# An earlier and thinner token list between attention and a mixture of experts

## The chip, the cores and the metric

The program runs on one core of a Trainium2 chip, in one launch. A core has five engines that run their own queues in order: TensorE (PE in the profile; its weight loads are PEld), VectorE (DVE), ScalarE (ACT), GpSimd (POOL) and SyncE (SP, which here only issues DMAs and reads a few registers). The metric is the device time in microseconds (us), the median of several runs.

## The reference

```python
def _attn_ref(q, k, v):                      # q, k, v: 8 x 8 x 1152 x 64
    q_pool = q.reshape(B, H, S // 2, 2, D).mean(axis=3)
    scores = np.matmul(q_pool, k.transpose(0, 1, 3, 2)) / np.sqrt(D)
    attn = np.exp(scores - scores.max(-1)); attn /= attn.sum(-1) + 1e-09
    return np.matmul(attn, v)
def _moe_ref(x, modality_id, w_gate, modality_bias, w1, w2):   # x: 4608 x 512, 8 experts of 1024
    logits = x @ w_gate + modality_bias[modality_id]
    e_idx = np.argmax(logits, axis=1)        # one expert for each token
    gate_w = softmax(logits)[tokens, e_idx]
    for e in range(E):
        mask = e_idx == e
        out[mask] = gate_w[mask, None] * (np.maximum(x[mask] @ w1[e], 0.0) @ w2[e])
```

Attention runs for 64 heads with pooled queries; its 4608 output rows are the tokens, and each goes through the one expert that its gate picks.

## The kernel before

**Attention.** The 64 heads are worked as 32 pairs (two heads side by side on the 128 partitions). The loop in `attention` has 18 steps a pair. Each step issues scores, the low halves of the exponentials, value products of earlier scores, and the maxima of the pair to come. For the reader of the trace: `L903`/`L904` are the score products, `L905` the exponentials on ScalarE (24 a pair), `L886`/`L888` the low halves `Pl` on ScalarE and VectorE, `L962` to `L964` the value products, `L836`/`L837` the maxima of the next pair (product, then VectorE reduction), `L803` the row of maxima, `L807` its transpose on TensorE and `L817` the DMA that puts the row in place.

What a later pair needs is prepared a pair or two ahead: GpSimd adds the query halves (`L655`), casts them (`L664`), takes the differences `lo` (`L692`, three a pair) and scales the values to `VH` (`L783`, two a pair: half 1 at step 3, half 0 at step 4). VectorE makes `VS` (`L795`, step 6) and `vl` (`L779`) from `VH`. Four of these GpSimd instructions are held: `hold` makes them wait for a certain VectorE instruction, so that they don't run beside it.

**Order.** The engines PE, ACT, DVE and POOL run in the order in which the code issues, step by step; SP's DMAs are ordered by a scheduler, unless `issue_after` puts one behind another. The list `side` holds generators (`route`, `first_list`, `other_list`); each is taken up after the one before it has ended, one `yield` at a time, at the end of a step. The number yielded is the count of steps to the next piece.

**Routing and lists.** Tokens come in four groups of eight pairs each. When a group is complete, `route(g)` picks each token's expert (one hot in `oh`), its gate (`gt`, stored to DRAM) and its place among its expert's tokens (`pos`). After the third group's routing `first_list` runs: the first `NA` = 6 blocks of 256 tokens are given to experts (`first_blocks`, `ownA`: the owner of each block), `place` works out each token's row in its block, and `listing` turns the rows into a list of token numbers by products of one-hot matrices (`ol`: which lane, `r`: which column). It works over 3 x 9 columns of 128 tokens. What is left of it when the last pair begins is drained in `gather_first`, just ahead of the first gather.

**Experts.** A block gathers its tokens from DRAM (`gather_x`, two indirect DMAs on GpSimd), multiplies by the first weights (`gemm1`) and the second (`gemm2`), and scatters. The first block's tokens and its four first weight quarters are fetched during attention's last pairs, into buffers of attention (`raw...`): `gather_first` and `load_first`, at the steps `T_G0` and `T_W0` counted from the start of pair 31. Their split into halves runs at the steps `T_W1` = (6, 4, 10, 11) of pair 31. The owner of a block is read by SP from `ownA` (`value_load`).

Of the kernel before, what the change touches and what calls it, by code (L numbers as in the profile page):

```python
# [42 lines left out]
BANK = W3 // 4  # L43
T_LIST = -127
PL = 2
RS = (4, 4, 2, 2)
SLOW_P = 1
# [41 lines left out]
JOBS = (8,)  # L89
T_G0 = -1  # L90
T_X0 = 7
# [27 lines left out]
NF = 4  # L119
T_W0 = (1, 3, 2, 3)  # L120
W1D = 0
# [42 lines left out]
class Router:  # L164
# [11 lines left out]
    def setup(self, ids, w_gate, bias):  # L176
# [40 lines left out]
        nc.sync.dma_start(out=self.xs[T - NT * P:T, DM:XW].rearrange("(t p) d -> p t d", p=P), in_=z)  # L217
        self.pos = con.tile([P, NTT], F32, name="pos")
        self.exp = con.tile([P, NTT], F32, name="exp")

# [56 lines left out]
    def route(self, g, eng):  # L277
# [45 lines left out]
        nc.vector.tensor_scalar(gt[:, :, 0], gt[:, :, 0], ts2[:, 0:1], 1.0 / WSC ** 2, op0=ALU.mult, op1=ALU.mult)  # L323
        nc.gpsimd.tensor_copy(gt[:, :, 1], ts2[:, 1:2].broadcast_to([P, NT]))
        eng.dma_start(out=self.xs[g * NT * P:(g + 1) * NT * P, DM:XW].rearrange("(t p) d -> p t d", p=P), in_=gt)
        yield rs
# [126 lines left out]

    def place(self, nt, late):

        nc, sm = self.nc, self.sm
        be = lambda a: a.unsqueeze(1).broadcast_to([P, nt, E])
        yield
        wide = lambda i: sm.tile([P, nt, E], F32, name=f"ohp{nt}_{i}") if late else sm.tile([P, 3, NT, E], F32, name=f"wide{i}").rearrange("p q t e -> p (q t) e")
        oh = wide(0)  # L460
# [13 lines left out]
        yield from pick(lim, self.na)  # L474
        yield from pick(row, self.full if late else self.cumA[:, 0:E])
        nc.vector.tensor_tensor(row, row, self.pos[:, 0:nt], op=ALU.add)
        if late:
            yield from pick(ok, self.done)
            nc.vector.tensor_tensor(ok, self.pos[:, 0:nt], ok, op=ALU.is_ge)
            more = new("more")  # L480
            yield from pick(more, self.half)
            nc.vector.tensor_tensor(more, more, ok, op=ALU.mult)
            nc.vector.tensor_tensor(row, row, more, op=ALU.add)
        nc.vector.tensor_tensor(ok, self.pos[:, 0:nt], lim, op=ALU.is_ge if late else ALU.is_lt)
        yield
# [13 lines left out]
        yield  # L499
        nc.vector.tensor_single_scalar(self.hi, self.hi, -float(2 * T // P), op=ALU.add)  # L500

    def operands(self, g, n, out):
# [63 lines left out]
    def first_list(self):  # L566

        for _ in self.first_blocks():
            yield 1
        for _ in self.place(3 * NT, False):  # L570
            yield PL
        yield T_LIST
        acc = self.con.tile([P, 2, 2 * NA], F32, name="accA")
        yield from self.listing(3, 2 * NA, acc)
        self.idxA = self.indices(2 * NA, acc, "A")

    def other_list(self):
        yield from self.other_blocks()
        yield from self.place(4 * NT, True)
        acc = self.con.tile([P, 2, 2 * (NBF - NA) + E], F32, name="accB")  # L580
        yield from self.listing(4, 2 * (NBF - NA) + E, acc)
        self.idxB = self.indices(2 * (NBF - NA) + E, acc, "B")


def attention(tc, ctx, att, ident, npairs, xpool, on_two, on_split, on_scale, jobs, side, set_pm, started, ahead, hip):
# [213 lines left out]
    def row(p, mp, u0, u1):  # L799

        n = u1 - u0
        m9 = sm.tile([P, 9], F32, name="m9")
        nc.vector.tensor_reduce(m9[:, 0:n], mp[:, u0:u1], op=ALU.max, axis=AX.X, negate=True)  # L803

        def finish():
            pt = some(0) if p else small()
            nc.tensor.transpose(pt[0:n, 0:P], m9[:, 0:n], ident)  # L807
            if now[0] > NSTEP:
                later_end(FD, lambda: put(pt))
            else:  # L810
                put(pt)

        def put(pt):
            mr = sm.tile([9, P], F16, name="mr", bufs=1)
            made.add((p, f"row{u1}"))
            nc.vector.tensor_scalar(mr[0:n], pt[0:n, 0:P], 1.0 / ROW, 16.0 * math.log(PSC) / ROW, op0=ALU.mult, op1=ALU.add)
            done = (nc.sync if p or u0 else nc.scalar).dma_start(out=B2[p % 2][D:D + 1, 2 * S + u0 * P:2 * S + u1 * P], in_=mr[0:n])  # L817
            if turns:
                with tc.issue_after(done.ins):
                    while turns:  # L820
                        turns.pop(0)()
        return finish
# [172 lines left out]

    turns = []
    now, flushed = [0], [-1]
# [133 lines left out]
    if ahead:  # L1131
        last = (npairs - 1) * NSTEP
        room = []

        def early():
# [37 lines left out]
    for t in range(NSTEP * npairs, NSTEP * npairs + 40):  # L1173
# [4 lines left out]
        ends(t)  # L1178
    assert not any(todo.values()) and not any(at_end.values())


# [10 lines left out]
def gather_x(nc, rt, j, tile_):  # L1192

    x = []
    for h in parts(j):
        x.append(tile_(h))
        nc.gpsimd.indirect_dma_start(out=x[h][:, :], out_offset=None, in_=rt.xs[0:3 * NT * P if j < NA else T, :],
                                     in_offset=bass.IndirectOffsetOnAxis(ap=index(rt, j, h)[0], axis=0))
    return x
# [22 lines left out]

def experts(tc, ctx, rt, ident, pre, w1, w2, out, side, first):

# [43 lines left out]
    def load_w(j, q):  # L1268
# [3 lines left out]
        if e is None:  # L1272
            own, k = (rt.ownA, j) if j < NA else (rt.ownB, j - NA) if j < NBF else (rt.ownH, j - NBF)
            e = b["e"] = nc.sync.value_load(own[0:1, k:k + 1], min_val=0, max_val=E - 1)
        if q < 4:
# [249 lines left out]
def attention_moe(tc, att, ids, w_gate, bias, w1, w2, out):  # L1525
    nc = tc.nc
    with ExitStack() as ctx:
# [9 lines left out]
        def on_two(n, x2):  # L1537
# [29 lines left out]
        def load_first(q, tile_):  # L1567
            if not q:
                first["e"] = nc.sync.value_load(rt.ownA[0:1, 0:1], min_val=0, max_val=E - 1)
# [10 lines left out]
        with ExitStack() as c2:  # L1580
            c2.enter_context(tc.manual_schedule(engines=MANUAL))
            attention(tc, c2, att, ident, NPAIR, xpool, on_two, on_split, rt.token_scale, jobs, side, set_pm, lambda: rt.setup(ids, w_gate, bias), ahead, hip)
# [6 lines left out]
        experts(tc, ctx, rt, ident, pre, w1, w2, out, rest(), first)  # L1589

# [43 lines left out]
```

## Time and profile before

| what | us |
|---|---|
| median of 3 runs | 1129.57 |
| runs, lowest and highest | 1128.46, 1130.51 |
| the profiled execution | 1128.8 |
| its span, first to last instruction | 1127.1 |
| PE busy | 1104.4 |
| DVE busy | 973.7 |
| ACT busy | 912.5 |
| POOL busy | 416.2 |

The span leaves out what lies around the instructions. A row of a table of windows gives, for a stretch of the span, its length, then for each engine the busy time and the number of instructions that begin in it, the granted TensorE clock, the busy share of the DMA engines and what they moved in GB/s. A row of a timeline gives start, duration, engine, line of the kernel, operation, what it writes and reads, and in brackets how long the engine was idle before it and what ended that. A row of the waits gives the total, the number and the longest wait of an engine for another. A row of a group of instructions gives count, busy time and mean duration in ns.

### The profile page before, as it was taken

Reading aid. Unit: us, or ns where it says so; the run is one execution under the profiler, and the core shown is the slowest. Engines: PE = TensorE matmul, PEld = TensorE weight load, DVE = VectorE, ACT = ScalarE, POOL = GpSimd, SP = SyncE. Lnnn points to the kernel's source line nnn. Section 1 sums busy time; section 2 is a strip of 40 time slices with the busy share of each in tenths; the row PEclk is TensorE's granted clock in tenths of the full one; section 3 lists DMA queues with packets and bytes.
Section 4 is the critical chain, followed back from the end, with each engine's and each line's share of the span. In section 5 each row is a group of like instructions: output and inputs, shape, how many; then the busy total and the mean of one; then the engine's idle time right before and its main releaser. Section 6 shows DMA issues by size and latency. Waiting matters only on the chain. (4 is left out here: it accounts for less than half of the span.)

```text
span 1127.1 us, 36928 instructions
## 1 busy us (share of the span) xinstructions
PE 1104.4 (98%) x15117; PEld 813.9 (72%) x15117; DVE 973.7 (86%) x1968; ACT 912.5 (81%) x1462; POOL 416.2 (37%) x408
## 2 busy tenths in 40 slices
PE   8999999999999999999999999999999999999997
PEld 3777777777777777777777777767667667667665
DVE  7999999999999999999999999887986666756754
ACT  5999999999999999999999998865646666655654
POOL 7753344355434444443444343123113112122111
PEclk9999999999999999999999999999999999999999
DMA  7767757768769678678687573599989999999993
GB/s 233 189 177 173 192 160 185 193 154 185 177 161 207 158 179 179 172 173 198 165 188 167 148 166 76 172 292 282 282 259 260 279 317 271 275 278 263 287 276 107
DMA packets 175522, 232.67 MB, mean 206 GB/s; under 512 B 92303, under 2 KB 126751, under 8 KB 175344
## 3 DMA queue, kind: packets, MB, share of 16 engines
q1 hardware_dynamic: 169254, 210.45, 71.2%
q0 software_dynamic: 6080, 19.78, 6.9%
q8 instruction: 120, 1.97, 0.8%
q14 instruction: 58, 0.48, 0.1%
q10 hardware_dynamic: 10, 0.00, 0.0%
HBM read 146.11 MB, written 18.99 MB: 146 GB/s over the span
## 5 line engine op out<-in xcount | busy, mean ns | idle before, releaser
L905 ACT ACTIVATE Pe<-psc 128x432 int32<-128x432 f32 x768 | 376.6, 526 | 40.8 <-PE psc L904 32.4
L837 DVE TENSOR_REDUCE mp<-pm 128x1 f32<-128x512 f32 x566 | 371.6, 684 | 16.0 <-PE pm L836 9.2
L962 PE MATMUL xp<-VH,Pe 128*128 128x65 f16 x2880 | 372.9, 194 | 0.0
L964 PE MATMUL xp<-VS,Pl 128*128 128x65 f16 x2880 | 372.1, 193 | 0.4 <-DVE Pl L888 0.4
L963 PE MATMUL xp<-vl,Pe 128*128 128x64 f16 x2880 | 371.0, 192 | 0.0
L963 PEld LDWEIGHTS <-Pe 128*128 128x128 f16 x2880 | 267.6, 98 | 87.7
L903 PE MATMUL psc<-B 128*128 128x432 f16 (+2 forms) x1152 | 304.3, 286 | 1.6 <-ACT Pe L905 1.4
L904 PE MATMUL psc<-B 65*128 65x432 f16 (+2 forms) x1152 | 304.9, 287 | 0.1
L962 PEld LDWEIGHTS <-Pe 128*128 128x128 f16 x2880 | 271.9, 98 | 42.0 <-issue 4.3
L964 PEld LDWEIGHTS <-Pl 128*128 128x128 f16 x2880 | 266.6, 97 | 0.6 <-DVE Pl L888 0.5
L886 ACT ACTIVATE Pl<-Pe 128x1152 f16<-128x1152 uint16 (+1 forms) x190 | 219.3, 1154 | 6.0
L836 PE MATMUL pm<-hi,QB 128*128 128x512 f16 x566 | 214.0, 379 | 4.1 <-DVE mp L837 2.9
L1309 PE MATMUL ph<-xpart,w1h 128*128 128x256 f16 x544 | 148.4, 273 | 0.0
L1311 PE MATMUL ph<-xpart,w1l 128*128 128x256 f16 x544 | 148.4, 273 | 0.0
L1310 PE MATMUL ph<-xpart,w1h 128*128 128x256 f16 x544 | 148.3, 273 | 0.0
L783 POOL TENSOR_SCALAR VH<-rawv,sc 128x512 f16<-128x512 f32 (+1 forms) x60 | 103.6, 1736 | 76.3 <-PE pm L836 35.6
L904 PEld LDWEIGHTS <-B 65*128 65x128 f16 x1152 | 112.9, 98 | 25.1 <-issue 2.4
L903 PEld LDWEIGHTS <-B 128*128 128x128 f16 x1152 | 112.6, 98 | 7.9 <-issue 2.5
L1315 DVE SCALAR_TENSOR_TENSOR hl<-ph,hh 128x512 f16<-128x512 f32 x72 | 49.7, 690 | 75.8 <-ACT hh L1314 75.7
L1314 ACT ACTIVATE hh<-ph 128x512 f16<-128x512 f32 x72 | 43.0, 598 | 87.3 <-PE ph L1311 87.3
L1403 PE MATMUL po<-w2l,hh 128*128 128x512 f16 x288 | 109.2, 379 | 0.0
L1404 PE MATMUL po<-w2h,hl 128*128 128x512 f16 x288 | 109.2, 379 | 0.0
(276 smaller groups left out, 1894.4 us busy)
## 6 DMA issues: line engine op xcount, KB each, us to landing
w2r<-in_w_dram SPq DMA_DIRECT2D x76, 512.0 KB
w1r<-in_w_dram SPq DMA_DIRECT2D x72, 512.0 KB
rawv<-in_att_dram SPq DMA_DIRECT2D x32, 576.0 KB
B<-hi SPq DMA_DIRECT2D x128, 144.0 KB
rawq<-in_att_dram SPq DMA_DIRECT2D x31, 576.0 KB
rawk<-in_att_dram SPq DMA_DIRECT2D x31, 576.0 KB
B<-qh SPq DMA_DIRECT2D x128, 72.0 KB
B<-lo SPq DMA_DIRECT2D x64, 144.0 KB
```

The source lines that it names most:

```text
L836: nc.tensor.matmul(pm, QB[p % 2][:, u], s["hi"][:, t * 512:(t + 1) * 512], start=True, stop=True)
L837: nc.vector.tensor_reduce(mp[:, u, t:t + 1], pm, op=ALU.max, axis=AX.X)
L886: nc.scalar.activation(low, rest, AF.Copy, scale=LOW)
L903: nc.tensor.matmul(o, b1[:, ks], b1[:, qs], start=True, stop=False, skip_group_check=True)
L904: nc.tensor.matmul(o, b2[:, ks], b2[:, qs], start=False, stop=True, skip_group_check=True)
L905: nc.scalar.activation(Pe[:, D + x0:D + x1], pt, AF.Exp, scale=1.0 / 16)
L962: nc.tensor.matmul(out, Ph[:, qs], vh[:, c, j, 0:D + 1], start=c == 0 and g == 0, stop=False, skip_group_check=True)
L963: nc.tensor.matmul(out[:, 0:D], Ph[:, qs], vl[:, c, j], start=False, stop=False, skip_group_check=True)
L964: nc.tensor.matmul(out, Pl[:, qs], vs[:, c, j, 0:D + 1], start=False, stop=c == NKC - 1, skip_group_check=True)
L1309: nc.tensor.matmul(o, hi[:, c, fs], xh[:, :, c], start=c == 0, stop=False)
L1310: nc.tensor.matmul(o, hi[:, c, fs], xl[:, :, c], start=False, stop=False)
L1311: nc.tensor.matmul(o, lo[:, c, fs], xh[:, :, c], start=False, stop=c == 3)
```

## The change

The first list is made from two groups of tokens, not three (`GA` = 2), so `first_list` follows `route(1)`, and `route(2)` waits in `side` until the list is done. It is issued in single steps: the blocks every 4 steps (`FB`), the places every 5 (`PL`), the listing every 3 (`OL`). `place_first` does part of the work on GpSimd and takes the one-hot that the routing has kept (`ohs`). `list_first` compares lane by lane, one column of 128 tokens at a time (18 compares of 128x128 in place of 9 of 128x384), and has the products with token numbers made by GpSimd. The low halves that pairs 26 and 27 gave to ScalarE (`P_LIST`) go back to VectorE. The routing is spread a little more (`RS`). The gather of the first tokens moves from one step ahead of pair 31 to fifteen steps ahead (`T_G0`), without a drain; two of the four first weight loads move to steps 4 and 5 of pair 30, behind the DMA of pair 30's row, and the other two stay, behind pair 31's row. The owners of blocks 1 to 5 are read behind pair 31's row.

```diff
-T_LIST = -127
-PL = 2
-RS = (4, 4, 2, 2)
+PL = 5
+RS = (5, 5, 4, 2)
+GA = 2
+FB = 4
+OL = 3
-P_LIST = {26: 0, 27: 0}
+P_LIST = {}
-T_G0 = -1
+T_G0 = -15
-T_W0 = (1, 3, 2, 3)
+T_W0 = (-13, -14, 2, 3)
...
-        oh = sm.tile([P, NT, E], BF16, name="oh16")
+        oh = self.ohs[:, ts] if g < GA else sm.tile([P, NT, E], BF16, name="oh16")
...
+    def place_first(self):
+        nc, sm = self.nc, self.sm
+        nt, g = GA * NT, nc.gpsimd
+        pos = self.pos[:, 0:nt]
+        of = sm.tile([P, 2, E], F32, name="of")
+        g.tensor_scalar(of[:, 0], self.na, float(TB), None, op0=ALU.mult)
+        g.tensor_scalar(of[:, 1], self.cumA[:, 0:E], float(TB), None, op0=ALU.mult)
+        both = sm.tile([P, 2, nt], F32, name="limrow")
+        for i in range(2):
+            w = sm.tile([P, nt, E], F32, name=f"wf{i}")
+            g.tensor_tensor(w, self.ohs, of[:, i].unsqueeze(1).broadcast_to([P, nt, E]), op=ALU.mult)
+            yield PL
+            nc.vector.tensor_reduce(both[:, i], w, op=ALU.add, axis=AX.X)
+            yield PL
+        lim, row = both[:, 0], both[:, 1]
+        ok = sm.tile([P, nt], F32, name="okf")
+        nc.vector.tensor_tensor(ok, pos, lim, op=ALU.is_lt)
+        g.tensor_tensor(row, row, pos, op=ALU.add)
+        g.tensor_scalar(row, row, float(2 * T), None, op0=ALU.add)
+        g.tensor_tensor(row, row, ok, op=ALU.mult)
+        yield PL
...
+    def list_first(self, n, acc):
...
+                nc.vector.tensor_tensor(o, self.hi[:, ts]..., self.col[:, 0:n]..., op=ALU.is_equal)
+                yield OL
+                for t in range(NT):
+                    j = k * NT + t
+                    nc.vector.tensor_scalar(ols[t // 3][:, t % 3], self.lane16, self.lo[:, j:j + 1], None, op0=ALU.is_equal)
+                    yield OL
+                    if t == 1:
+                        g.tensor_tensor(r[:, 0], o, self.tile1[:, ts]..., op=ALU.mult)
+                    if t == 4:
+                        g.tensor_scalar(r[:, 1], o, self.part, None, op0=ALU.mult)
...
     def first_list(self):
         for _ in self.first_blocks():
-            yield 1
-        for _ in self.place(3 * NT, False):
-            yield PL
-        yield T_LIST
+            yield FB
+        yield from self.place_first()
         acc = self.con.tile([P, 2, 2 * NA], F32, name="accA")
-        yield from self.listing(3, 2 * NA, acc)
+        yield from self.list_first(2 * NA, acc)
...
+            rows[p] = done.ins
...
-            at(last + T_W0[i], 0, lambda i=i: ahead[2](i, room[i]))
+            at(last + T_W0[i], 0, lambda i=i: behind(rows[npairs - 1 if T_W0[i] > 0 else npairs - 2], lambda: ahead[2](i, room[i])))
...
-            e = b["e"] = nc.sync.value_load(own[0:1, k:k + 1], min_val=0, max_val=E - 1)
+            with tc.issue_after(last_row) if j < NA else ExitStack():
+                e = b["e"] = nc.sync.value_load(own[0:1, k:k + 1], min_val=0, max_val=E - 1)
...
-                if g == 2:
+                if g == GA - 1:
                     side.append(rt.first_list())
...
         def gather_first(tile_):
-            while side:
-                drain(side.pop(0))
```

Three places in the order, with the line numbers of each kernel. First GpSimd in pair 30, before (`VH_125` is the value product for pair 31, half 1 and half 0; `lo` are the differences for pair 31):

```order
L664 CAST qh<-rawq 128x576
L692 TENSOR_TENSOR lo<-rawq,qh 128x576
L692 TENSOR_TENSOR lo<-rawk,hi 128x576 x2
L783 TENSOR_SCALAR VH_125<-rawv,sc 128x8x64
L783 TENSOR_SCALAR VH_125<-rawv,sc 128x10x64
L1197 DMA rawq<-xs,giA 128x514 x2
```

The same place after the change (`L739` is the cast, `L767` the differences, `L858` the value product, `L1278` the gather; `sx`, `ts` and `gt` belong to the third group's gates):

```order
L739 CAST qh<-rawq 128x576
L767 TENSOR_TENSOR lo<-rawq,qh 128x576
L767 TENSOR_TENSOR lo<-rawk,hi 128x576
L321 TENSOR_SCALAR sx<-sx 128x9
L322 TENSOR_SCALAR ts_17081<-ts_17081 128x1
L327 COPY gt<-ts_17081 128x9
L767 TENSOR_TENSOR lo<-rawk,hi 128x576
L858 TENSOR_SCALAR VH_125<-rawv,sc 128x8x64
L1278 DMA rawq<-xs,giA 128x514 x2
L858 TENSOR_SCALAR VH_125<-rawv,sc 128x10x64
```

The two gathers now stand between the two value products, and the gate's operations of the third group behind two differences. Second, VectorE in pair 29 around the row of maxima, before (`L845` is the last reduction of the maxima, `L803` the row, `ol` and `o` belong to the list):

```order
L512 TENSOR_TENSOR ol_16983<-lof,lane_1088 128x384
L837 TENSOR_REDUCE mp<-pm 128x1
L845 TENSOR_REDUCE mp<-pm 128x4
L888 TENSOR_SCALAR Pl_116<-Pe_115 128x576
L274 TENSOR_TENSOR lg<-pm,lg 128x216
L837 TENSOR_REDUCE mp<-pm 128x1 x2
L518 TENSOR_TENSOR o_17097<-hif,col 128x108
L845 TENSOR_REDUCE mp<-pm 128x1
L803 TENSOR_REDUCE m_17134<-mp 128x9
```

And after (`L913` and `L921` are the reductions, `L964` the low half, `L878` the row; `L324` reads what GpSimd's `L322` writes):

```order
L913 TENSOR_REDUCE mp<-pm 128x1
L921 TENSOR_REDUCE mp<-pm 128x4
L964 TENSOR_SCALAR Pl_116<-Pe_115 128x576
L316 TENSOR_REDUCE sx<-wide_16376 128x9
L319 TENSOR_REDUCE ts_17081<-scales 128x1
L277 TENSOR_TENSOR lg<-pm,lg 128x216
L913 TENSOR_REDUCE mp<-pm 128x1 x2
L324 RECIPROCAL ts_17081<-ts_17081 128x1
L325 RECIPROCAL gt<-sx 128x9
L326 TENSOR_SCALAR gt<-gt,ts_17081 128x9
L921 TENSOR_REDUCE mp<-pm 128x1
L878 TENSOR_REDUCE m_17161<-mp 128x9
```

List operations have left this place, and those of the third group's gates stand there. Third, SP between the row of pair 30 and the copies for pair 31, after the change (`L892` is the row's DMA, `L1649` reads an owner, `L1651` loads a weight quarter, `L700` copies for pair 31):

```order
L892 DMA B_0_111<-mr 1x9x128
L700 DMA B_1_113<-lo 64x1152
L1649 TENSOR_LOAD ownerA
L1649 ISA x2
L1651 ISA
L1651 DMA rawk<-in_w_dram 128x1024
L700 DMA B_17392<-qh 64x576
L700 DMA B_1_113<-qh 64x576
```

Before, the row and the copies followed each other here, and all four weight loads stood behind the row of pair 31.

More of the change, by code (lines that the diff above doesn't have):

```diff
@@ L452, in other_blocks, with place @@
         self.done, self.full, self.half = done, full, half
-    def place(self, nt, late):
+    def place(self, nt):
         nc, sm = self.nc, self.sm
@@ L458, in place @@
         yield
-        wide = lambda i: sm.tile([P, nt, E], F32, name=f"ohp{nt}_{i}") if late else sm.tile([P, 3, NT, E], F32, name=f"wide{i}").rearrange("p q t e -> p (q t) e")
+        wide = lambda i: sm.tile([P, nt, E], F32, name=f"ohp{nt}_{i}")
         oh = wide(0)
@@ L474, in place @@
         yield from pick(lim, self.na)
-        yield from pick(row, self.full if late else self.cumA[:, 0:E])
+        yield from pick(row, self.full)
         nc.vector.tensor_tensor(row, row, self.pos[:, 0:nt], op=ALU.add)
[L477 to L484, printed above, removed]
+        yield from pick(ok, self.done)
+        nc.vector.tensor_tensor(ok, self.pos[:, 0:nt], ok, op=ALU.is_ge)
+        more = new("more")
+        yield from pick(more, self.half)
+        nc.vector.tensor_tensor(more, more, ok, op=ALU.mult)
+        nc.vector.tensor_tensor(row, row, more, op=ALU.add)
+        nc.vector.tensor_tensor(ok, self.pos[:, 0:nt], lim, op=ALU.is_ge)
         yield
@@ L578, in other_list @@
         yield from self.other_blocks()
-        yield from self.place(4 * NT, True)
+        yield from self.place(4 * NT)
         acc = self.con.tile([P, 2, 2 * (NBF - NA) + E], F32, name="accB")
@@ L994, in evac @@
             later(XD, lambda: split_x(p, x2))
-    turns = []
+    turns, rows = [], {}
     now, flushed = [0], [-1]
@@ L1133, in attention, with behind @@
         room = []
+        def behind(ins, fn):
+            with tc.issue_after(ins):
+                fn()
         def early():
@@ L1179, in attention @@
     assert not any(todo.values()) and not any(at_end.values())
+    return rows[npairs - 1]
 def index(rt, j, h):
@@ L1196, in gather_x @@
         x.append(tile_(h))
[L1197 removed]
+        nc.gpsimd.indirect_dma_start(out=x[h][:, :], out_offset=None, in_=rt.xs[0:GA * NT * P if j < NA else T, :],
                                      in_offset=bass.IndirectOffsetOnAxis(ap=index(rt, j, h)[0], axis=0))
@@ L1220, in turn, with experts @@
             nc.vector.tensor_tensor(xl[:, h, 2 * q:2 * q + 2], px[:, h], xh[:, h, 2 * q:2 * q + 2], op=ALU.subtract)
-def experts(tc, ctx, rt, ident, pre, w1, w2, out, side, first):
+def experts(tc, ctx, rt, ident, pre, w1, w2, out, side, first, last_row):
     nc = tc.nc
@@ L1567, in load_first @@
         def load_first(q, tile_):
-            if not q:
+            if "e" not in first:
                 first["e"] = nc.sync.value_load(rt.ownA[0:1, 0:1], min_val=0, max_val=E - 1)
@@ L1581, in attention_moe @@
             c2.enter_context(tc.manual_schedule(engines=MANUAL))
-            attention(tc, c2, att, ident, NPAIR, xpool, on_two, on_split, rt.token_scale, jobs, side, set_pm, lambda: rt.setup(ids, w_gate, bias), ahead, hip)
+            last_row = attention(tc, c2, att, ident, NPAIR, xpool, on_two, on_split, rt.token_scale, jobs, side, set_pm, lambda: rt.setup(ids, w_gate, bias), ahead, hip)
         def rest():
@@ L1588, in rest @@
                 yield from g
-        experts(tc, ctx, rt, ident, pre, w1, w2, out, rest(), first)
+        experts(tc, ctx, rt, ident, pre, w1, w2, out, rest(), first, last_row)
 _OUTS = [((T, DM), 'float32')]
```

40 lines of the change are left out of this document (added).

## The prediction

> **What bounds the kernel.** I read the page first, then a table of windows, then the waits.
>
> ```profile
> span 1127.1 us, 36928 instructions
> PE 1104.4 (98%) x15117; PEld 813.9 (72%) x15117; DVE 973.7 (86%) x1968; ACT 912.5 (81%) x1462; POOL 416.2 (37%) x408
> PE   8999999999999999999999999999999999999997
> PEclk9999999999999999999999999999999999999999
> ```
>
> TensorE (PE) is busy all the way at the full granted clock, so only stretches in which it starves can give time back. The profiled execution took 1128.8 us, 0.8 under the median of 1129.57; the sum below is made against 1128.8 and then put on the median. To find the starved stretches I cut the attention stage at the starts of pairs, two pairs to a window. A window holds 48 exponentials (L905), 24 a pair; the second table gives all engines; the third is one of equal windows from the experts.
>
> ```profile
> 467.12:510.88 43.76, 23.41 (x48) 1.00 0.74 178
> 598.71:645.79 47.08, 23.25 (x48) 1.00 0.68 167
> ```
>
> ```profile
> 422.79:467.12 44.33, 44.28 (x775) 34.30 (x772) 43.24 (x105) 42.05 (x74) 20.52 (x19) 1.00 0.76 176
> 467.12:510.88 43.76, 43.76 (x765) 33.96 (x762) 41.80 (x92) 41.69 (x73) 18.60 (x14) 1.00 0.74 178
> 554.66:598.71 44.05, 44.05 (x766) 34.14 (x763) 42.27 (x96) 41.88 (x75) 20.63 (x19) 1.00 0.74 177
> 598.71:645.79 47.08, 45.57 (x784) 35.19 (x783) 44.79 (x117) 44.17 (x76) 21.98 (x20) 1.00 0.68 167
> 645.79:692.36 46.57, 44.31 (x753) 33.80 (x750) 45.85 (x109) 42.51 (x74) 17.75 (x13) 1.00 0.50 115
> 692.36:732.78 40.42, 38.79 (x757) 32.03 (x754) 35.97 (x87) 35.79 (x68) 8.60 (x6) 1.00 0.55 161
> ```
>
> ```profile
> 775.00:800.00 25.00, 25.00 (x174) 16.09 (x173) 22.09 (x62) 15.83 (x20) 5.20 (x5) 1.00 0.98 271
> ```
>
> Columns: window, length, then busy time and count of PE, weight loads, VectorE (DVE), ScalarE (ACT) and GpSimd (POOL). Two quiet pairs (20 and 21) take 43.76 us, PE without a gap. Pairs 18 and 19, which carry most of the second routing, take 0.57 more with 13 more DVE instructions, and PE still hardly stops: that is PE's own added work. Pairs 24 to 29 carry the third routing and most of the first list: 0.29, 3.32 and 2.81 over, 6.4 together. The experts keep PE full (25.00 of 25.00, and nines in the page's slices to the last but one), so an earlier start of the experts moves the end by as much.
>
> ```profile
> PE pm L836 <- DVE mp L837: 1.7, 4, 0.5
> PE pm L807 <- DVE m L803: 1.3, 2, 1.0
> PE psc L903 <- ACT Pe L905: 0.9, 2, 0.5
> PE pm L844 <- DVE mp L837: 0.9, 1, 0.9
> ```
>
> ```profile
> ACT w1h L1575 <- DMA rawk<-in_w_dram: 0.8, 1, 0.8
> ```
>
> These are PE's waits from 576 to 733 and ACT's from 692 on: DVE holds PE up, mostly through the maxima and, once a pair, through the row (L803, then the transpose L807). The last line is the first expert weight landing late.
>
> **The list, thinned and moved.** Counted in the order, the new list has 45 DVE instructions: 12 for the blocks, 6 for the places, 2 column masks, 18 compares, 2 sums and 5 for the indices. By the yields they run from step 4 of pair 20 to step 4 of pair 28, some 5 or 6 a pair. Priced by the routing's rows, 1.44 us of busy DVE for 13 instructions (43.24 less 41.80) is 0.11 each, so 5.0 us over four windows, 1.25 each, beside 1.96 us in which DVE is idle in a quiet window. The cover is that idle time. The bounds are 0 and, should each take what the nearest row says with nothing overlapped, 45 x 0.27 = 12.2 us, 3.0 a window, 1.1 too much in each.
>
> ```profile
> L524 DVE TENSOR_SCALAR r<-o,part 128x108 bf16<-128x108 f32 x3 | 0.8, 270 | 0.0
> L512 DVE TENSOR_TENSOR ol<-lof,lane 128x384 bf16<-128x384 bf16 x9 | 5.6, 622 | 0.0
> L291 POOL TENSOR_TENSOR wide<-bias,inv 128x72 f32<-128x72 f32 x1 | 0.3, 309 | 0.1
> ```
>
> I take 0.11, because the routing is the same kind of small work in the same place and its windows are measured. PE keeps 18 small products and the routing: pairs 28 and 29 now carry the third routing, priced as 18 and 19 at 0.57, and the rest of the list gets 0.25 a window for four windows. So 6.4 goes and 1.6 comes back. ScalarE gets 4 low halves less (P_LIST); it is not what PE waits for there, 0. The 13 new GpSimd instructions (0.3 to 0.45 us each by the L291 row) stand in idle stretches of GpSimd, which is busy 18.6 of 43.8; only in pair 24 do two of them stand ahead of a value product, some 0.6 us against the 0.54 of slack that the gathers' rows below show: 0, at most 0.1.
>
> **The port.** GpSimd and DVE hold each other up in this trace:
>
> ```profile
> 658.16 1.28 POOL L692 TENSOR_TENSOR lo<-rawk,hi 128x576 f16<-128x576 f32 x1 [0.98 <-DVE Pl L888]
> 658.68 1.18 DVE L512 TENSOR_TENSOR ol<-lof,lane 128x384 bf16<-128x384 bf16 x1
> 660.88 1.28 POOL L692 TENSOR_TENSOR lo<-rawk,hi 128x576 f16<-128x576 f32 x1 [1.43 <-ACT hi L676]
> 660.92 1.55 DVE L888 TENSOR_SCALAR Pl<-Pe 128x576 f16<-128x576 uint16 x1
> ```
>
> L512 took 1.18 us where the other eight of its group take 0.55 (9 x 0.622 less 1.18), and L888 1.55 instead of the 0.45 of the row in the next part, each until the GpSimd operation had ended. One of 9 list compares met one. With 18 compares and 13 GpSimd operations I count three or four meetings, some 2 us of DVE, of which idle time takes most: 0.5 us. Bounds: 0, and the second rival. [...]
>
> **The third routing's new wait.** In the order of DVE, the reciprocals of the gate (L324) now stand two instructions ahead of the row's maximum in pair 29, and wait for GpSimd's L322, which stands behind two held differences. In a quiet odd pair these places are:
>
> ```profile
> 544.83 1.28 POOL L692 TENSOR_TENSOR lo<-rawk,hi 128x576 f16<-128x576 f32 x1 [0.39 <-DVE Pl L888]
> 546.16 0.28 DVE L845 TENSOR_REDUCE mp<-pm 128x1 f32<-128x128 f32 x1
> 546.47 0.18 DVE L803 TENSOR_REDUCE m<-mp 128x9 f32<-128x27 f32 x1
> 546.89 0.27 PE L807 MATMUL pm<-ident,m 128*9 128x128 f32 x1
> 547.29 0.45 DVE L888 TENSOR_SCALAR Pl<-Pe 128x576 f16<-128x576 uint16 x1
> ```
>
> GpSimd is free at 546.11 and needs some 0.7 for L321 and L322 (0.35 each by the L291 row); DVE would be there at 546.16, so it waits 0.6 and then does 0.45 of gates before the maximum. PE has 0.24 of slack (546.65 to 546.89). Of the 0.8 I take 0.6, between 0 (the maxima's buffers cover it) and 1.1 (no slack, 0.6 and 0.45).
>
> **The gathers.** In GpSimd's order the two gathers now stand between the two value products of pair 31, and DVE's VS waits for the second:
>
> ```profile
> 697.15 3.43 POOL L783 TENSOR_SCALAR VH<-rawv,sc 128x512 f16<-128x512 f32 x2 [10.09 <-PE pm L836]
> 701.12 0.46 DVE L795 TENSOR_SCALAR VS<-VH 128x1152 f16<-128x1152 f16 x1
> 706.62 0.18 DVE L803 TENSOR_REDUCE m<-mp 128x9 f32<-128x27 f32 x1
> 706.85 0.28 PE L807 MATMUL pm<-ident,m 128*9 128x128 f32 x1 [0.29 <-DVE m L803]
> 713.36 1.44 POOL L1197 DMA_INDIRECT rawq<-xs,giA  x1 [12.79 <-DVE siA L563]
> 715.10 1.06 POOL L1197 DMA_INDIRECT rawq<-xs,giA  x1 [0.30 <-issue]
> ```
>
> The products end at 700.58, 0.54 ahead of VS; two gathers take 2.8 (713.36 to 716.16). VS, and behind it in DVE's queue the maxima of pair 31, come 2.3 late. Up to the row's maximum two list instructions fall away (some 0.7), so PE waits 1.3 more at the transpose, where it has no slack. Bounds: 0 (three buffers of maxima cover it) and 2.3. The 0.29 that PE waits there now goes with the list.
>
> **The weights.** Two of the four first loads are issued behind the row of pair 30, a pair earlier, where DMA is half idle (0.50 in the window row). ACT's wait of 0.8 for the first weight ends, and with it one of PE's two waits for exponentials (0.5). The drain of the list at the start of pair 31 goes too. I take 0.6 for both, between 0.2 and 1.0.
>
> ```profile
> L1274 SPq TENSOR_LOAD <-ownerA x5: 262/264/280, 634.1 to 636.4; - x5
> ```
>
> ```profile
> 690.19 1.10 SPq L625 DMA_DIRECT2D B<-qh  x2
> 726.71 3.03 SPq L1280 DMA_DIRECT2D w2r<-in_w_dram  x4
> ```
>
> SP reads one owner ahead of the early loads and five behind the late ones, 0.6 us each (5 from 634.1 to 636.4). Behind the first stand the copies for pair 31, issued from 690 on for a pair that starts at about 713; behind the five stand loads that can't be issued before 726. So 0. That SP no longer reads owners in pair 27 is worth 0 as well: no PE wait names a DMA.
>
> **Sum.** -6.4 +1.6 +0.5 +0.6 +1.3 -0.3 -0.6 = -3.3: 1125.5 for the profiled execution, 1126.3 for the median. A change under 0.2% (2.3 us: 1127.3 to 1131.8) can't be told from none.
>
> **Rivals.**
> 1. *No free room.* DVE's work costs wherever it stands. Pairs 26 to 29 paid 6.1 us for 7.0 us of more DVE (2.99 and 4.05), 0.87 each; the list's 5.0 and the routing's 1.44 would then cost 5.6 instead of 1.6, and the time is 1130.3: no change. For it: DVE is busy 41.80 of 43.76 us. Against it: pairs 18 and 19 took 1.44 without a stop of PE.
> 2. *The port, on the slower side.* Each of the 18 compares meets a GpSimd operation as L512 did: 18 x 0.63 = 11.3 us in pairs 24 to 27, about 1 of it covered, the rest at 0.87: 9.0 instead of 0.5, 1134.8. It turns slower from 13 meetings on. GpSimd is busy 18.6 of 43.8 us, and 1 in 9 met before, so it is unlikely. [...]
> 3. *Dearer gathers.* DVE is dense in pair 30, where the rows of the gathers are from a time of little DVE. At twice 2.8 us VS comes 5.1 late, PE pays 4.1 instead of 1.3, and the time is 1129.1: no change. [...]
> 4. *VS is covered* and the routing's wait too: 1126.3 - 1.9 = 1124.4.
>
> **How the numbers follow.** My case 0.55 (its own range 1124.8 to 1128.0), rival 1 0.17, rival 2 0.05, rival 3 0.11, rival 4 0.12. The range leaves out rival 2, half of rival 1 and the far end of rival 4: 1123.8 to 1129.8. Faster: nine tenths of my case and rival 4, 0.62; slower 0.06; the rest, 0.32, no change.
>
> **What would show it.** Pairs 24 to 29 should come to about 133.5 us in place of 137.7, pairs 20 to 23 to at most 88.3 (twice 43.76 now). VS in pair 30 should start right behind a value product that ends some 2 us later than now, with PE waiting over 1 us at its row; the wait of ACT for the first weight should be gone. The prediction is wrong if pairs 20 to 27 each grow by half a microsecond, if compares often take over 0.5 us, or if pairs 30 and 31 grow by more than 1 us together.

## The result: slower by 1.1%, and the profile after

The changed kernel takes 1141.98 us (median, 1140.42 to 1144.64) against 1130.04 for the kernel before beside it: a ratio of 1.0109, with a 95% interval of 1.0097 to 1.0121. The forecast was 1126.3.

The page of the changed kernel, its span, busy times and two rows of its slices:

```profile
span 1140.1 us, 36924 instructions
PE 1108.7 (97%) x15108; PEld 816.2 (72%) x15108; DVE 983.1 (86%) x1965; ACT 915.1 (80%) x1458; POOL 418.2 (37%) x421
PE   8999999999999999999999999999999999999997
PEclk9999999999999999999999999999999999999999
```

The span is 13.0 us longer, and PE's busy time has grown by only 4.3: two thirds of the loss is PE standing still. About 1 us of the 13.0 lies ahead of the first exponential (19.39 us in place of 18.42), a start that ranges from 18.21 to 19.58 over the kernels below. The same windows as before, two pairs each, from pairs 18 and 19 on; the last ends inside pair 31 (length, then busy time and count of PE, weight loads, DVE, ACT and POOL, the clock, DMA):

```profile
425.55:471.89 46.34, 44.97 (x775) 34.54 (x772) 45.06 (x104) 42.96 (x75) 19.92 (x19) 1.00 0.72 168
471.89:516.79 44.90, 44.23 (x765) 34.14 (x762) 44.05 (x103) 42.16 (x74) 18.75 (x14) 1.00 0.72 173
516.79:563.01 46.22, 44.11 (x765) 34.01 (x762) 42.72 (x100) 42.21 (x73) 21.31 (x21) 1.00 0.75 169
563.01:609.82 46.81, 44.93 (x765) 34.46 (x762) 45.96 (x102) 42.72 (x73) 20.61 (x18) 1.00 0.67 166
609.82:656.20 46.38, 44.71 (x777) 34.46 (x774) 45.43 (x103) 42.64 (x73) 19.84 (x16) 1.00 0.72 168
656.20:703.04 46.84, 44.87 (x775) 34.56 (x772) 45.22 (x108) 42.37 (x75) 21.46 (x23) 1.00 0.52 121
703.04:746.00 42.96, 40.03 (x735) 32.70 (x733) 34.36 (x76) 35.91 (x68) 8.97 (x7) 0.96 0.53 147
```

Each of the first six is 1.1 to 3.1 us above the quiet 43.76. The first is the second routing alone, without any list: 46.34 where it had been 44.33. Only the fifth and the sixth come near what stood there before (47.08 and 46.57). PE's waits from 247 to 746 name three places:

```profile
PE pm L882 <- DVE m L878: 6.0, 6, 1.6
PE pm L912 <- DVE mp L913: 3.4, 5, 2.0
PE psc L980 <- DMA B<-mr: 2.1, 1, 2.1
```

L882 is the transpose of the row of maxima, L912 a product for the maxima, and the third line is PE waiting for the DMA that puts a row in place: a wait that the kernel before did not have at all. The transpose is held up by this, here in pair 24, between VS (L870) and the row (L878):

```profile
571.56 0.91 DVE L870 TENSOR_SCALAR VS<-VH 128x1152 f16<-128x1152 f16 x1
574.00 1.28 POOL L767 TENSOR_TENSOR lo<-rawq,qh 128x576 f16<-128x576 f32 x1 [1.85 <-issue]
574.38 1.03 DVE L558 TENSOR_TENSOR o<-lohif,col 128x108 f32<-128x108 f32 x1
577.06 1.28 POOL L767 TENSOR_TENSOR lo<-rawk,hi 128x576 f16<-128x576 f32 x1 [1.77 <-DVE Pl L964]
577.50 0.89 DVE L562 TENSOR_SCALAR ol<-lane,lohif 128x128 bf16<-128x128 bf16 x1
578.62 0.18 DVE L878 TENSOR_REDUCE m<-mp 128x9 f32<-128x27 f32 x1
578.86 0.28 PE L882 MATMUL pm<-ident,m 128*9 128x128 f32 x1 [1.56 <-DVE m L878]
```

Two list instructions (L558 takes 0.45 where nothing meets it, L562 0.24 to 0.26) start 0.38 and 0.44 us behind a GpSimd difference and end with it. VS to row takes 7.06 us here and 4.84 in the quiet even pairs 12, 14 and 16 of the same trace; in those DVE stands idle for 0.03 us of the 4.84. PE pays 1.56. Some 0.46 of the 7.06 is VS itself, 0.91 us in place of 0.45 beside the cast (L739); in the run below that moves the two list instructions away that part stays, and PE's wait is 0.04.

### The profile page after: what moved, and what is told of

It is laid out like the page before. It is cut to its first block, busy times and chain, and to the rows that moved or that the text cites. A ratio compares the mean times of both kernels' runs of the same rounds, so it can differ in the third digit from the quotient of the medians.

```text
span 1140.1 us, 36924 instructions
## 1 busy us (share of the span) xinstructions
PE 1108.7 (97%) x15108; PEld 816.2 (72%) x15108; DVE 983.1 (86%) x1965; ACT 915.1 (80%) x1458; POOL 418.2 (37%) x421
## 5 line engine op out<-in xcount | busy, mean ns | idle before, releaser
L981 ACT ACTIVATE Pe<-psc 128x432 int32<-128x432 f32 x768 | 381.0, 527 | 51.8 <-PE psc L980 42.8
L913 DVE TENSOR_REDUCE mp<-pm 128x1 f32<-128x512 f32 x566 | 372.3, 684 | 16.7 <-PE pm L912 10.1
L962 ACT ACTIVATE Pl<-Pe 128x1152 f16<-128x1152 uint16 x186 | 216.5, 1164 | 5.9
L912 PE MATMUL pm<-hi,QB 128*128 128x512 f16 x566 | 214.0, 379 | 6.5 <-DVE mp L913 4.6
L858 POOL TENSOR_SCALAR VH<-rawv,sc 128x512 f16<-128x512 f32 (+1 forms) x60 | 103.7, 1737 | 65.9 <-PE pm L912 29.8
L964 DVE TENSOR_SCALAR Pl<-Pe 128x576 f16<-128x576 uint16 (+1 forms) x198 | 105.5, 533 | 5.8 <-ACT Pe L981 4.7
```

The lines of the kernel that those rows point to most:

```text
L912: nc.tensor.matmul(pm, QB[p % 2][:, u], s["hi"][:, t * 512:(t + 1) * 512], start=True, stop=True)
L913: nc.vector.tensor_reduce(mp[:, u, t:t + 1], pm, op=ALU.max, axis=AX.X)
L962: nc.scalar.activation(low, rest, AF.Copy, scale=LOW)
L981: nc.scalar.activation(Pe[:, D + x0:D + x1], pt, AF.Exp, scale=1.0 / 16)
```

## The experiments

Pair lengths below are the distances between the first exponentials of neighbouring pairs (24 exponentials a pair), taken from each kernel's profile. A gain is the difference between a run's median and the 1141.98 of the changed kernel, which was taken at another time; the kernel before, run beside each, had medians from 1129.96 to 1130.86, so a gain is good to a microsecond or two, and the pair lengths say where it lies.

### What one spare instruction costs, step by step

The kernel before in three versions, each with one spare instruction in nine pairs (the compare of the list, or a sum):

```
+DUM = (77, 114, 151, 224, 261, 298, 371, 408, 445)     # 18 * pair + step
         ends(t)
+        if t in DUM:
+            HOOK['f']()
...
+        HOOK['f'] = lambda: nc.vector.tensor_scalar(rt.hx, rt.lane16, rt.part, None, op0=ALU.is_equal)
# the sum:           nc.vector.tensor_reduce(rt.hy, rt.before, op=ALU.add, axis=AX.X)
```

> The kernel before, with one spare compare of 128x128 (the list's, 0.24 us alone) put into one step of each of nine quiet even pairs: step 5 in pair 4, 6 in 6, 7 in 8, 8 in 12, 9 in 14, 10 in 16, 11 in 20, 12 in 22, 13 in 24. Nothing else is changed. Theory of the place: pairs 12 and 20 (steps 8 and 11, beside the differences) grow by 0.5 to 0.8 us each, the pairs of steps 6, 7, 9, 10 and 12 by 0 to 0.1, and steps 5 and 13 by nothing; 1.0 to 1.6 in all. Theory of the room: each of the nine pairs grows by about 0.2 us, 0.87 of 0.24, 1.9 in all.

> As the kernel before with a spare instruction in nine even pairs at steps 5 to 13, but the instruction is a sum of 128x72 to 128x9 in f32 (0.2 us alone) in place of the compare. If the price at steps 8, 10 and 11 is that of the GpSimd difference holding an element-wise instruction, and sums are not held (in the trace of the kernel after none of them was slowed), pairs 12, 16 and 20 grow by 0 to 0.15 and the nine together by under 0.6. If it is the place alone, they grow as they did with the compare, by 0.5 each, 2.0 in all.

> As the kernel before with the spare compare of 128x128, but in odd pairs: step 5 in pair 3, 6 in 9, 7 in 17, 8 in 5, 9 in 7, 10 in 13, 11 in 15, 12 in 21, 13 in 23. In odd pairs the logits' sum stands in the same stretch, so the differences start at other times against the steps. Theory of the place: at most two of the nine compares are held (0.8 to 0.95 us) and cost 0.5 to 0.7 each; the others cost 0 to 0.25. Theory of the room: 0.2 each.

| step | compare, even pair: took / pair grew | sum, even pair: took / pair grew | compare, odd pair: took / pair grew |
|---|---|---|---|
| 5 | 0.79 / 0.31 | 0.23 / 0.00 | 0.79 / 0.31 |
| 6 | 0.24 / 0.13 | 0.21 / 0.11 | 0.24 / 0.17 |
| 7 | 0.24 / 0.00 | 0.22 / 0.01 | 0.24 / 0.23 |
| 8 | 0.95 / 0.54 | 0.22 / 0.00 | 0.24 / 0.16 |
| 9 | 0.24 / 0.00 | 0.22 / 0.01 | 0.24 / 0.00 |
| 10 | 0.89 / 0.47 | 0.22 / 0.01 | 0.24 / 0.00 |
| 11 | 0.89 / 0.48 | 0.22 / 0.01 | 0.24 / -0.06 |
| 12 | 0.23 / 0.00 | 0.21 / 0.01 | 0.23 / 0.12 |
| 13 | 0.27 / 0.00 | 0.22 / 0.00 | 0.25 / see below |

The whole executions took 1133.3, 1129.0 and 1131.2 us (one time each; the kernel before beside them had medians of 1130.9, 1130.7 and 1130.7). The second kernel of the three has the sum, the third the compare in odd pairs. Pairs 3 to 6 have waits of their own in the kernel before, and at step 5 it is GpSimd's value product (`VH`), not a difference, that the compare starts 0.05 us behind. Behind each of the three dear steps the next pair grew by another 0.10 to 0.11 us, though of these only pair 13 is steady elsewhere. In pairs 22 and 23 of the third kernel a wait for a row's DMA (1.13 us) covers the reading of step 13. The first kernel with the compare at step 8, then at step 9, and the second with the sum at step 8:

```profile
303.33 1.29 POOL L698 TENSOR_TENSOR lo<-rawq,qh 128x576 f16<-128x576 f32 x1 [2.21 <-issue]
303.71 0.95 DVE L1563 TENSOR_SCALAR hx<-lane,part 128x128 bf16<-128x128 bf16 x1
307.30 0.28 PE L813 MATMUL pm<-ident,m 128*9 128x128 f32 x1 [0.61 <-DVE m L809]
...
349.68 0.24 DVE L1563 TENSOR_SCALAR hx<-lane,part 128x128 bf16<-128x128 bf16 x1
349.84 1.28 POOL L698 TENSOR_TENSOR lo<-rawk,hi 128x576 f16<-128x576 f32 x1 [0.82 <-DVE Pl L894]
```

```profile
301.71 1.28 POOL L698 TENSOR_TENSOR lo<-rawq,qh 128x576 f16<-128x576 f32 x1 [2.22 <-issue]
302.09 0.22 DVE L1563 TENSOR_REDUCE hy<-before 128x9 f32<-128x72 f32 x1
```

For the even pairs the theory of the room falls: the same instruction costs nothing at steps 7, 9, 12 and 13, and 0.5 (0.6 with the pair behind it) at 8, 10 and 11. The nine pairs together grew by 1.9 us, just what that theory had said; it is the spread over the steps that it has wrong. What makes the difference is the GpSimd difference: a compare that starts behind it (step 8, by 0.38 us) ends with it and takes 0.95 us, one that starts 0.16 ahead of it (step 9) takes 0.24, and a sum in the same place (step 8, 0.38 behind) takes 0.22 and costs nothing. I had expected steps 5 and 10 to be free. In odd pairs room is not free everywhere: a compare that nothing holds costs 0.16 and 0.17 us in pairs 5 and 9 (steps 8 and 6). The readings of pairs 15, 17 and 21 mean little: 15 and 17 range over 0.4 and 0.3 us between kernels that have the same instructions there, and pair 21 grew by 0.46 in the second kernel, without a spare instruction of its own.

### The list and the routing off three steps

```
+        if side and t >= wait and not p % 2 and c18 in (8, 10, 11):
+            due = due or t
-        if side and t >= wait:
+        elif side and t >= wait:
+            t, due = due or t, None
```

> The kernel after, with only the pieces of routing and list that fall on steps 8, 10 and 11 of an even pair run one or two steps later (step 9 or 12); the pieces behind them stay where they were, and GpSimd's order is unchanged. Eight VectorE instructions move: two in each of pairs 10, 18 and 24, one in 20, two in 26 (and one sum). Theory of the place: PE's waits at the row's transpose in these pairs (0.75, 0.75, 0.57, 1.56, 1.42) fall to 0.1 or less each, and the time is 4.5 to 5.0 us less, about 1137.2. Theory of the room: VectorE has the same work, so no change, 1142.

Measured: 1136.49 us (1134.01 to 1138.27), 5.5 less than the changed kernel. PE's waits at the row's transpose fell from 0.75, 0.75, 0.57, 1.56 and 1.42 to 0.17, 0.18, 0, 0.04 and 0 us. Of its waits from 471 to 740 the one at the transpose that stays is that of pair 29:

```profile
PE pm L912 <- DVE mp L913: 2.9, 2, 2.0
PE psc L980 <- DMA B<-mr: 1.8, 2, 1.6
PE pm L882 <- DVE m L878: 1.0, 1, 1.0
```

The work is the same, instruction by instruction, and GpSimd's order too; ten DVE instructions stand one or two steps later, seven of them element-wise and three reductions (the expectation's eight was a miscount), and two of ScalarE's with them. The four runs spread over 4.3 us. In the profiled one, the fastest, the pairs 10, 11, 18 to 21 and 24 to 27 are 7.0 us shorter, 2.4 of it in 10, 11, 18 and 19, where no list stands. So some 5 us of the loss were place, not room.

### The routings at their old steps

```
-RS = (5, 5, 4, 2)
+RS = (4, 4, 4, 2)
-        yield 2
+        if g >= GA: yield 2
...
     def first_list(self):
+        yield 10
```

> The kernel after, with only the first two routings at the steps they had before (spacing 4 in place of 5, no pause ahead of the gate's DMA); the list starts where it did. Theory of the place (a thin VectorE instruction costs little, but not between VS and the row of maxima, and least of all while a GpSimd difference runs): pairs 10, 11, 18 and 19 lose the 0.95 + 1.07 + 0.95 + 1.05 us that they gained, PE's waits of 0.75 us at the row's transpose in pairs 10 and 18 go, and the time is 4.0 us less, 1138.0. Theory of the room (VectorE's work costs the same wherever it stands): as many instructions as in the kernel after, so no change, 1142.

Measured: 1137.58 us (1136.98 to 1137.71), 4.4 less. Pairs 10 and 11 went from 46.35 back to 44.34 us, pairs 18 and 19 from 46.34 to 44.53, and the waits of 0.75 are gone. In the changed kernel this stood in pair 10:

```profile
258.37 1.29 POOL L767 TENSOR_TENSOR lo<-rawq,qh 128x576 f16<-128x576 f32 x1 [2.22 <-issue]
258.74 1.00 DVE L306 SCALAR_TENSOR_TENSOR wide<-wide,ieE 128x72 f32<-128x72 f32 x1
```

That is step 8 again. For the odd pairs 11 and 19 (1.07 and 1.05 us) the visible waits make up 0.48; the rest I can't put to an instruction.

### The places' GpSimd work behind the cast

```
     def place_first(self):
+        yield 6
...
-            yield PL
+            yield PL - (i == 0)
             nc.vector.tensor_reduce(both[:, i], w, op=ALU.add, axis=AX.X)
-            yield PL
+            if i: yield PL
```

> The kernel after, with only three of the GpSimd instructions of the places (and the one VectorE sum that reads them) moved from step 4 to step 10 and 14 of pair 22, behind the cast of the query and two differences. Theory of the queue: the three (1.2 us) delay the cast, the cast SyncE's copies and the next load, and the row of pair 22 lands behind 1.2 MB of loads and stores; then PE's wait of 2.07 us for the row's DMA at the start of pair 23 goes and the time is 2.1 us less, 1139.9. Rival: the DMA queue is as full in any case and the row is late by chance of that pair; then no change.

Measured: 1138.82 us (1138.57 to 1141.01), 3.2 less. PE's wait for the row at the start of pair 23 is gone, and pairs 20 to 23 fell from 91.12 to 88.94 us. The chain, in the changed kernel, on GpSimd and on SP's queue:

```profile
522.69 1.88 POOL L858 TENSOR_SCALAR VH<-rawv,sc 128x640 f16<-128x640 f32 x1
524.55 0.24 POOL L511 TENSOR_SCALAR of<-na 128x8 f32<-128x8 f32 x1
524.75 0.24 POOL L512 TENSOR_SCALAR of<-cutA 128x8 f32<-128x8 f32 x1
524.95 0.72 POOL L516 TENSOR_TENSOR wf<-ohs,of 128x144 f32<-128x144 bf16 x1
525.62 0.89 POOL L739 CAST qh<-rawq 128x576 f16<-128x576 f32 x1
526.53 1.10 SPq L700 DMA_DIRECT2D QB<-qh  x2
527.73 0.54 SPq L233 DMA_DIRECT2D xs<-x  x1
529.11 1.19 SPq L715 DMA_DIRECT2D rawq<-in_att_dram  x1
532.13 0.80 SPq L892 DMA_DIRECT2D B<-mr  x1
539.42 0.34 PE L980 MATMUL psc<-B 65*128 65x432 f16 x1 [2.07 <-DMA B<-mr]
```

Three small instructions push the cast back by 1.1 us, the cast pushes the copies, and the store (L233) and the load (L715), 576 KB each, come nearer to the row of 2.2 KB behind them. Against the run with the three moved, the store and the load stand 0.8 and 0.3 us nearer. The row was issued at once and landed 7 us later. The wait at this place is 1.17 to 2.07 us in the four profiles that have the three instructions here with the list, and 0 to 0.26 in the six that have them later (though 1.13 once without any list, in the third kernel with spare compares). Pair 30 is 1.3 us shorter in this run's profile by the clock alone (below); by the pair lengths 2.2 belong to pairs 20 to 23.

### The gathers behind both value products

```
-T_G0 = -15
+T_G0 = -14
```

> The kernel after, with only the two first gathers moved one step on, behind both value products of pair 31 in GpSimd's order. If the growth of pair 30 (20.40 to 23.92 us) is VS waiting for the second product, VS starts some 2.7 us earlier against the start of its pair, PE's wait of 2.0 at the maxima goes, and the time is 2.5 to 3.5 us less, about 1139. Rival: a running gather holds VectorE by itself, wherever it stands; then the instructions behind VS are held for it instead, and under 1 us comes back.

Measured: 1139.43 us (1139.20 to 1139.93), 2.5 less; pair 30 fell from 23.92 to 20.75, 1.3 of it the clock (below), and a wait of 0.41 us at the row's transpose is left. In the changed kernel:

```profile
707.97 1.58 POOL L858 TENSOR_SCALAR VH<-rawv,sc 128x512 f16<-128x512 f32 x1 [10.90 <-PE pm L912]
709.74 1.22 POOL L1278 DMA_INDIRECT rawq<-xs,giA  x1 [0.18 <-issue]
711.26 0.98 POOL L1278 DMA_INDIRECT rawq<-xs,giA  x1 [0.30 <-issue]
712.28 2.23 POOL L858 TENSOR_SCALAR VH<-rawv,sc 128x640 f16<-128x640 f32 x1
714.54 0.58 DVE L870 TENSOR_SCALAR VS<-VH 128x1152 f16<-128x1152 f16 x1 [1.78 <-POOL VH L858]
715.78 0.38 PE L912 MATMUL pm<-hi,QB 128*128 128x512 f16 x1 [2.01 <-DVE mp L913]
```

The gathers took 2.5 us together (709.74 to 712.24), about as in the kernel before. One low half on DVE (L964) took 1.16 us in place of 0.45 beside the second of them; with the gathers moved, VS ran beside the first in 0.45. So in this one place a gather seems to have held DVE, but that was not the price: the rival falls.

### The edits together, and further

> The kernel after with the three edits of the first runs together: the first two routings at their old steps, the gathers behind both value products, the three GpSimd instructions of the places later. If they are three separate places, the gains add up: 4.4 + 2.5 + 3.2 = 10.1 us less than the kernel after, 1131.9, and PE's waits for a row's DMA at pair 23 and for the maxima in pair 30 are gone. Rival: they share a cover (the row's DMA waits in one case for what another delays), then 6 to 8 us come back, 1134 to 1136.

Measured: 1133.30 us (1132.05 to 1134.37), 8.7 less than the changed kernel, where the parts sum to 10.1. By the profile both named waits are gone but for 0.1 us at pair 23; pair lengths give 8.9. The slow clock of pair 30, 1.3 us in the profile, went both with the places and with the gathers and can go only once, which would account for the 1.4 that is missing.

> The three edits together and the moved pieces of even pairs (steps 8, 10 and 11 left free) as well: the first two routings at their old steps, the gathers behind both value products, three GpSimd instructions of the places later, and the list off the three steps. What the moved pieces gave in pairs 20 to 27, where the three edits changed nothing (0.50 + 0.14 + 1.58 + 0.49 + 1.34 + 0.59 = 4.6 us by the pair lengths), comes off 1133.3: 1128.7, about 0.2% faster than the kernel before. If the list's VectorE work cost room and not place, it stays at 1133.

Measured, with the edit of the three steps added: 1128.74 us, a ratio of 0.9990 (0.9981 to 0.9999) to the kernel before. That is the 1128.7 expected, 0.1% under the kernel before.

> The same four edits, and the third routing at the steps of the first two: it begins at step 10 of pair 29 in place of step 5 of pair 28, with spacing 4 and no pause ahead of the gate's DMA, and ends in pair 31. Theory of the place: pairs 28 and 29 fall from 23.24 and 23.60 to the quiet 21.6 and 22.3, pairs 30 and 31 gain at most 0.3 together, and the time is 2.6 to 2.9 us less than with the four edits, about 1126.0, 0.4% faster than the kernel before. Rival: the routing meets the split of the first weights in pair 31 and costs there what it cost before; then no change against the four edits, 1128.7.

```
-        yield 2
         eng.dma_start(out=self.xs[...], in_=gt)
...
         self.idxA = self.indices(2 * NA, acc, "A")
+        yield 23
```

Measured: 1126.79 us, a ratio of 0.9973 (0.9962 to 0.9984): faster than the changed kernel by 15.2 us, and than the kernel before by 0.3%. Its windows from pair 18 to pair 29:

```profile
422.78:467.10 44.32, 44.28 (x775) 34.30 (x772) 43.23 (x105) 42.09 (x74) 20.55 (x19) 1.00 0.74 176
...
555.30:600.06 44.76, 44.52 (x765) 34.27 (x762) 43.66 (x102) 42.27 (x73) 20.12 (x18) 1.00 0.73 174
600.06:644.51 44.45, 44.41 (x777) 34.42 (x774) 43.28 (x103) 41.99 (x74) 19.99 (x16) 1.00 0.72 175
644.51:689.66 45.15, 44.65 (x773) 34.41 (x770) 43.38 (x99) 42.00 (x73) 20.46 (x19) 1.00 0.56 129
```

The second routing is back at 44.32, and pairs 24 to 29 take 134.4 us, where the prediction had 133.5 and the changed kernel has 140.0.

> The four edits and the later third routing, and the five index instructions of the list, which stood together at step 4 of pair 28, one by one at steps 6, 7, 9, 12 and 13. At step 4 two of them are held for 0.35 us or more by a value product on GpSimd and the five take 1.6 us; pair 28 is 22.83 us long against a quiet 21.62. Theory of the place: pair 28 falls by 0.8 to 1.1 us and the time to about 1125.8. Theory of the room: no change, 1126.8.

Here each of the five index instructions got a `yield` of its own. Measured: 1127.40 us (1126.51 to 1128.00), 0.9971 (0.9959 to 0.9983). Pair 28 fell by 0.98 us as expected, but the time did not follow: in this execution PE waited 0.62 us for a row's DMA that came at once in the run above, and odd pairs 17, 19 and 23 were 0.2 to 0.4 us longer without a visible wait. A gain of 1 us is at the edge of what these runs can tell.

### The weights late again

```
-T_W0 = (-13, -14, 2, 3)
+T_W0 = (1, 3, 2, 3)
```

> The three edits of the first runs together, with the two early loads of first weights put back behind the row of pair 31, where they were in the kernel before. If the early loads are worth what the prediction gave them, ScalarE waits 0.8 us for a first weight again in pair 31 and the time is 0.4 to 0.8 us more than with the three edits, about 1133.9; if they are worth nothing, it stays at 1133.3.

Measured: 1137.36 us (1135.89 to 1138.52), 4.1 more than with the three edits: much more than either theory. The first line below is ScalarE's wait from 712 on, the second PE's, the third the read of the first owner on SP, the fourth a window that begins 0.95 us after PE's wait of 2.29:

```profile
ACT w1h L1655 <- DMA rawk<-in_w_dram: 2.7, 1, 2.7
```

```profile
PE psc L979 <- ACT Pe L981: 2.7, 2, 2.3
```

```profile
L1649 SPq TENSOR_LOAD <-ownerA x1: 1113/1113/1113, 715.1 to 715.1; - x1
```

```profile
726.76:730.17 3.41, 3.41 (x49) 2.49 (x46) 2.95 (x8) 2.08 (x4) 0.00 (x0) 0.50 0.02 5
```

In the kernel before the owner had been read in pair 27 and the first load was issued 2.2 us ahead of pair 31's start (710.50, 712.75). Here the read stands behind the row, and the first load goes out 0.7 us ahead of it (716.80, 717.48). Pair 31 to PE's end is 3.85 us longer than with the three edits: 2.29 are the wait, and the other 1.6 go with the clock, which fell to half for 3.4 us behind it. So the early loads are worth 4 us to this kernel. In the kernel before, late loads went with a wait of 0.8 on ScalarE and no fall of the clock (1.00 from 712.75 to 745); that the owner's read makes the difference fits the order, but no run moved it by itself.

## Why the prediction was wrong, step by step

- **What bounds the kernel, and what the list cost in its old place**: right. With the places mended, pairs 24 to 29 take 134.4 us in place of 137.7. That the total, 1126.79, stands beside the forecast of 1126.3 is in part luck: the forecast held 2.4 us for the port, the gates and the gathers (0.5, 0.6, 1.3) that this order avoids. The signs it named for being wrong came: pairs 20 to 25 each grew by 0.5 to 1.8 us (27 by 0.5; 26, which had held more of the list before, lost 1.2), five of 18 compares took over 0.5, and pair 30 grew by 3.5 while pair 31 gained only 1.0.
- **"The cover is that idle time"**: this step failed. 1.96 us of idle DVE in a window of two pairs is true, but none of it lies between VS and the row, where DVE runs for 4.8 us with 0.03 idle and the row has some 0.2 us of slack. The spacing of 3, 4 and 5 steps lays pieces on those steps by turns. The price of 0.11 from the routing came from pairs in which the pieces happened to miss the steps 8, 10 and 11: there each of its instructions took 0.15 to 0.39.
- **The port, 0.5**: mis-sized. No run shows a port; the runs show element-wise DVE instructions that start behind a GpSimd difference and end with it (0.94 us for one of 128x8), and a cost of some 5 us (1141.98 to 1136.49 with ten instructions moved); with the routing back at its old steps, the list's part of it is 4.6 (1133.30 to 1128.74). By the timeline fifteen instructions of routing and list took 0.5 to 1.05 us in place of 0.15 to 0.45, eight of them behind a difference and seven behind GpSimd's value product; five were compares. The prediction took a share (one compare in nine) where the step decides, and counted compares where other element-wise instructions of routing and list are held as well. Rival 2, at 0.05, had the meetings and a fair price of 0.55 a meeting (0.6 measured at the dear steps), though not the place: 5 of 18 compares met, and the other ten were routing, blocks, indices and a column mask. It was to turn slower from 13 meetings on. Rival 1, no free room, had 1130.3; it falls with the map of the even pairs and with the 1126.79 that the same work takes in better places. Rival 4 falls with the gathers.
- **The routing's spacing, which got no term at all**: 4.4 us, the second largest part of the loss, in pairs that hold no list. It overlaps with the port's: 2.4 of it came back when the pieces in pairs 10 and 18 were moved off the steps. What held up the odd pairs is only in part known.
- **GpSimd's 13 instructions, "0, at most 0.1"**: failed in pair 22, at 2.2 us by the pair lengths of pairs 20 to 23. I asked whether GpSimd had time, and looked only at the value products; what is queued behind them there is the cast, then SP's copies and a load, then the row.
- **The third routing's gates, 0.6**: mechanism right, size off. DVE waited 0.36 us for GpSimd's L322, but with the two sums and the three gate instructions ahead of the row PE waited 1.00. Moving that routing brought 2 us with all it had in pairs 28 and 29.
- **The gathers, 1.3**: right in kind and too small. VS started 11.50 us after the start of pair 30 (8.76 before), 2.7 late where 2.3 was forecast, and PE paid 2.0, with 1.3 of slow clock behind it. It paid not at the transpose, as forecast, but at a product of the maxima (L912), which waited for the first reduction behind VS; the list instructions that fell away had stood behind that reduction, so they did not pay for it. Rival 3 falls: the gathers took 2.5 us, not twice 2.8.
- **The weights, -0.6, and SP's reads, 0**: right. ScalarE waits for no weight any more, and from pair 31's first exponential to PE's end it is 407.05 us in place of 408.04 (the kernel before and its three versions with spare instructions range from 407.61 to 408.71 there, the kernels with the early loads from 407.01 to 407.81). The zero for the reads rests on the early loads alone.

## What to carry to other kernels

Before spreading small work over a loop, make the map: one spare instruction in each step of a quiet iteration shows in a single run which steps are free and which cost about twice the instruction (here 0.00 us at steps 7, 9, 12 and 13 and 0.47 to 0.54 at 8, 10 and 11, for a compare of 0.24). An engine's idle total said nothing on that here (1.96 us in two pairs, 0.03 between VS and the row); look for the stretch ahead of the wait in which it has none, and for what runs on the engine that can hold it. And price a small instruction on a side engine by what is queued behind it, through the DMA queue to the end.

## What the runs showed of the hardware

**Who is held.** The eight element-wise instructions of routing and list that were slowed behind a GpSimd difference in the changed kernel began 0.38 to 0.44 us behind its start and ended 0.03 to 0.13 us behind its end, whatever their size: 0.94 us for one of 128x8, 0.95 for one of 128x128. One that started 0.16 us ahead of a difference took 0.24 (step 9 of the first spare-compare kernel). Sums were not slowed: 0.21 to 0.23 us for the spare one in nine of nine places, and 0.67 to 0.69 for the reductions of the maxima (L913, 128x512) in all 62 places where one began behind a difference in the changed kernel, as elsewhere. Not every element-wise instruction is held either: over the traces of the kernel before and of the changed one the reciprocal `rr` of 128x5 took 0.19 to 0.20 us in all 51 places where it began behind a difference, and `x` of 128x320, which reads what PE's value products write, 0.55 to 0.56 in all 51. Behind GpSimd's own value product (L858, 1.88 us) it depended on the start: in the changed kernel two compares of 128x128 that began 0.05 and 0.06 us behind it ended 0.84 us after the product's start, one that began 0.79 behind took its own 0.26, and an index instruction (L636) that began 1.34 behind took 0.57 and ended with it.

**The clock behind a stall.** In the changed kernel PE stood for 2.01 us in pair 30, and 0.8 us after it had begun again its granted clock fell to half for 3.4 us; in the run with the places later a wait of 2.0 us at the same place left the clock whole. First the stretch of the changed kernel, then that of the other:

```profile
716.60:720.00 3.40, 3.40 (x42) 2.52 (x39) 2.81 (x6) 2.85 (x5) 0.00 (x0) 0.50 0.32 66
```

```profile
713.80:717.20 3.40, 3.40 (x62) 2.59 (x59) 3.37 (x9) 3.37 (x6) 0.00 (x0) 1.00 0.35 78
```

42 matmuls in place of 62: pair 30 took 23.92 us in the one and 22.64 in the other. The clock fell behind this wait in the run with the routings at their old steps too (0.50 from 711.20 to 714.20, pair 30 23.89 us), and behind the wait of 2.29 us with the late weights. In the changed kernel it stayed at 1.00 behind the wait of 2.07 us for the row at pair 23 and behind that of 1.56 in pair 24. So the length of the wait alone did not decide; what did is not shown.

**The row's DMA.** 2.2 KB landed 7 us after its issue behind 1.15 MB. Waits for such a row came and went between runs (1.13 us in pair 22 of the third spare-compare kernel, 0.62 and 0.66 ahead of pair 27 in two others) where nothing near them had been changed; their cause is open.
